# Two banks of sums, two groups in turn, keys loaded by tokens and a last group with tokens on partitions, in a fused attention and expert kernel

## The chip, the cores and the metric

One core of one Trainium2 chip. The metric is the device time of one execution in microseconds (us), lower is better. The profile's span, from the first to the last instruction, is 1.8 to 1.9 us shorter than that time.

## The reference

A polynomial-sketch attention without softmax feeds an expert layer with ELU. Sizes: 4 batches, 4 heads, 1088 tokens, head size 32, sketch size 8; 4352 tokens of 128 features into 2048 hidden units and back, all float32 (the sketches and the expert weights arrive as 64-bit floats and are rounded on the chip).

```python
def phi(x):
    a = np.einsum('rd,bhsd->bhsr', S1, x)
    b = np.einsum('rd,bhsd->bhsr', S2, x)
    return np.einsum('bhsi,bhsj->bhsij', a, b).reshape(*x.shape[:-1], r * r)
q_p, k_p = (phi(q), phi(k))
kv = np.einsum('bhsf,bhsd->bhfd', k_p, v)
z = np.sum(k_p, axis=2)
num = np.einsum('bhsf,bhfd->bhsd', q_p, kv)
den = np.einsum('bhsf,bhf->bhs', q_p, z)[..., None] + 1e-06
# ... (num / den), heads joined to 128 features = x; then
h = x @ w_in
g = np.where(h > 0.0, h, np.exp(np.minimum(h, 0.0)) - 1.0)
return (g @ w_out).astype(np.float32)
```

## The kernel before

Tokens go through in 9 groups: eight of 512 tokens and a last one of 256. For each group and each of 8 pairs of weight blocks, TensorE computes two hidden blocks (`mm1`, tile `h`), ScalarE and VectorE form ELU (`elu_a`, `elu_d`, tiles `e`, `gg`), and two steps later TensorE adds two products to the group's sum (`mm2`, tile `o`). One such pass is a step. The keys of a batch (`KF`, `KO`, `KA`), the queries of a group (`q1` to `q5`) and the rounding of the weights (`RA`, `RB`, `RC`) are hung between the steps. The kernel uses PSUM, the memory that matmuls write, in 8 banks: four for `h`, two for `aux`, one for `kv` (which also holds `wps`), one for `o`.

```python
def KF(b, gi):                       # key features of one group of tiles
    if gi < 2:
        abps[b] = psum.tile([P, 512], F32, name="abp", tag="aux")
    abp = abps[b] if gi < 2 else abps[b][:, 256:]      # the last tile shares the bank of gi == 1
    # ... matmuls into abp ...
    nc.scalar.copy(ab[...], abp[...])
# ...
def KA(b, gi):
    if gi == 0:
        kv_ps[b] = psum.tile([P, 4, 2 * D], F32, name="kv", tag="kv", bufs=1)
    # ... kv += kp.T @ v ...
def KZ2(b):
    wps = kv_ps[b][:, 2]
    nc.tensor.matmul(wps[:, :H * R], SX[:], zm[:]...)
    nc.vector.tensor_mul(SW[:, b, :, 2, :], wps[...], bmask...)
# ...
def mm2(g, cp, first, last):
    if first:
        ops[g] = psum.tile([P, 512], F32, name="o", tag="o", bufs=1)
    # ... two matmuls accumulate into ops[g] ...
def fin1(g, last):                   # partial sums of groups 0 and 1 go to SBUF and are added
    # ...
def fin2(g):                         # last group: transposes back to tokens
    # nc.tensor.transpose x2, nc.scalar.copy, two output DMAs, both from nc.sync
# ...
seg = [(g, r) for r in (range(0, 2), range(2, 4), range(4, NP)) for g in range(2)]
seg += [(g, range(NP)) for g in range(2, NQ)]
```

Of the kernel before, what the change touches and what calls it, by code (L numbers as in the profile page):

```python
# [27 lines left out]
def kernel(  # L28
# [50 lines left out]
    def load_v(eng, b):  # L79
        for u in range(2):  # L80
# [59 lines left out]

    hd["k", 0] = work.tile([P, 2, NT, D], F32, name="hd_k", tag="hd_k")
    for i, eng in enumerate((nc.sync, nc.scalar)):
        eng.dma_start(hd["k", 0][64 * i:64 * i + 64].rearrange("p c t d -> p (c t d)"),
                      k[0, 2 * i:2 * i + 2].rearrange("h (a x) d -> (h a) (x d)", a=32))
# [3 lines left out]
    load_hd(nc.sync, "q", q, 0, 0, 8)  # L148
# [37 lines left out]
    load_v(nc.sync, 0)  # L186
# [8 lines left out]
    for b in range(1, B):  # L195
        load_hd(nc.sync, "k", k, b, 0, NT)
        load_v(nc.sync, b)
        load_hd(nc.sync, "q", q, b, 0, NT)
# [16 lines left out]
    idle = psum.tile([P, 512], F32, name="idle", tag="o", bufs=1)  # L215
# [21 lines left out]
    Sab = const.tile([FD, H, 2 * R], F32, name="Sab")  # L237
    SW = const.tile([FD, B, H, 3, R], F32, name="SW")
    keep_warm(3)
    sps = psum.tile([P, 512], F32, name="sps", tag="aux")  # L240
    nc.tensor.matmul(sps[:, :2 * R], Sx[:].rearrange("p h d -> p (h d)"), ident[:2 * R, :2 * R])
    nc.vector.tensor_mul(Sab[:], _ap(sps[:, :2 * R], [[0, H], [1, 2 * R]]), _ap(bmask[:], [[1, H], [0, 2 * R]]))  # L242
    for b in range(B):
        nc.gpsimd.tensor_copy(SW[:, b, :, :2, :].rearrange("p h x r -> p h (x r)"), Sab[:])

# [7 lines left out]

    def outer(dst, ab):

        a_, b_ = ab[:, :, 1, :], ab[:, :, 0, :]
        nc.vector.tensor_mul(dst, _ap(a_, list(a_.ap[1:]) + [[0, R]]), _ap(b_, [b_.ap[1], [0, R], b_.ap[2]]))  # L257
# [3 lines left out]
    abps, kv_ps, feats, zms, kvz = {}, {}, {}, {}, {}  # L261

    def KF(b, gi):

        if gi < 2:
            abps[b] = psum.tile([P, 512], F32, name="abp", tag="aux")
        abp = abps[b] if gi < 2 else abps[b][:, 256:]
        tiles = KG[gi]
        n = len(tiles)
        rows = P if tiles[-1] + KT < NT else 64  # L270
        for j, i in enumerate(tiles):
            for u in range(rows // 64):
                nc.tensor.matmul(abp[64 * u:64 * u + 64, j * 64:j * 64 + 64], kT[b][:, u * KT + i, :],  # L273
                                 Sab[:].rearrange("p h y -> p (h y)"),
                                 skip_group_check=True, tile_position=(0, 64 * u))
        ab = work.tile([P, 4, H, 2, R], F32, name="ab", tag="ab", bufs=3)
        nc.scalar.copy(ab[:rows, :n].rearrange("p t h x r -> p (t h x r)"), abp[:rows, :n * 64])  # L277
        feats[b, gi] = ab, rows
# [9 lines left out]
    def KA(b, gi):  # L288
# [3 lines left out]
        if gi == 0:  # L292
            kv_ps[b] = psum.tile([P, 4, 2 * D], F32, name="kv", tag="kv", bufs=1)
# [12 lines left out]
    def KC(b):  # L306

        kv = kv_ps[b][:, :2, :D + 1]
# [15 lines left out]
    def KZ2(b):  # L324
        zm = zms.pop(b)
        wps = kv_ps[b][:, 2]
# [93 lines left out]
    def q5_first():  # L420
# [3 lines left out]
        RC(0)  # L424
# [13 lines left out]
        for tt in range(2):  # L438
            nc.vector.tensor_scalar(dn[:, tt], xps[tt][:, :, D], 1e-6, None, op0=ADD)
            nc.vector.reciprocal(dn[:, tt], dn[:, tt])  # L440
            nc.vector.tensor_mul(xn[:, tt], xps[tt][:, :, :D], _ap(dn[:, tt], [[1, 8], [0, D]]))
        for tt in range(2):
# [3 lines left out]
            nc.scalar.copy(xg[0][:, 256 * tt:256 * tt + 256], q[:, :256])  # L446
            if tt == 0:
                q1(1)
# [72 lines left out]
    def mm2(g, cp, first, last):  # L521
        n = qn[g] * P
        if first:
            ops[g] = psum.tile([P, 512], F32, name="o", tag="o", bufs=1)
# [5 lines left out]
    oT = {}  # L530

    def fin1(g, last):
        n = qn[g] * P
        o = ops.pop(g)[:, :n]
        if g in oT:
            nc.vector.tensor_add(oT[g][:, :n], oT[g][:, :n], o)
            o = oT[g][:, :n]
# [168 lines left out]
```

## Time and profile before

| | before |
|---|---|
| time | 299.99 us, median of 3 (299.66 to 300.33) |
| span of the profiled run | 296.4 us |
| TensorE busy; VectorE; ScalarE | 284.5 us (96%); 168.0 (57%); 188.1 (63%) |
| first `h` matmul, first `o` matmul | 19.75 us, 28.23 us |
| first `o` to the end of the last `o` | 262.98 us |
| end of the last `o` to the end of the span | 5.2 us |

The last three rows cut the span: a **head** until the first `o`, a **body**, and a **tail**. The prediction shows the slices, the chain and the head of TensorE's timeline. One view is not shown there, TensorE's waits from 26 us to the end (engine, line and tile, then who released it: total us, how often, the longest):

```profile
PE abp L273 <- ACT ab L277: 1.4, 3, 0.5
PE otp L559 <- DVE oT L543: 0.5, 1, 0.5
PE abp L273 <- DVE kT L233: 0.3, 1, 0.3
```

So in 270 us TensorE idles for four recorded holes in the body and one in the tail. Whatever the change wins in the body, it can win only from these 1.7 us.

### The profile page before, as it was taken

What the parts mean: (1) busy time and instruction counts of PE and PEld (TensorE: products, weight loads), DVE (VectorE), ACT (ScalarE), POOL (GpSimd) and SP (SyncE); (2) the same over time, 40 slices, a digit from 0 to 9 for tenths busy, and PEclk for the clock granted to TensorE, in tenths of its full rate; (3) what the DMA queues carried; (4) which work ended last, traced back from release to release, by engine and by line L of the source; (5) the groups of instructions that cost most, each with busy time, mean ns of one, the idle gap of its engine ahead of it and who ended that gap; (6) DMA issues with size and microseconds to landing.
All of it is one profiled execution on the core that took longest, in us unless ns stands there. A gap on an engine that the chain in (4) does not pass through costs nothing.

```text
span 296.4 us, 4034 instructions
## 1 busy us (share of the span) xinstructions
PE 284.5 (96%) x1448; PEld 146.0 (49%) x1448; DVE 168.0 (57%) x296; ACT 188.1 (63%) x355; POOL 19.0 (6%) x46
## 2 busy tenths in 40 slices
PE   6879989999999999999999999999999999999993
PEld 4854444544544653445544644444444444444682
DVE  4789999964657275425457274435543554355441
ACT  2249888566467467666646557766666686667681
POOL 1110034620000010000000100000000000000000
PEclk9799999999999999999999999999999999999998
DMA  6942999220110100011001100011002000110010
GB/s 157 339 157 88 198 208 217 39 75 0 18 20 9 30 0 0 3 16 19 1 2 16 21 0 0 1 18 19 0 0 31 8 0 1 17 21 0 6 30 18
DMA packets 37907, 13.37 MB, mean 45 GB/s; under 512 B 32768, under 2 KB 35968, under 8 KB 37888
## 3 DMA queue, kind: packets, MB, share of 16 engines
q1 hardware_dynamic: 37792, 12.84, 19.9%
q10 hardware_dynamic: 96, 0.28, 0.4%
q8 instruction: 11, 0.18, 0.3%
q14 instruction: 8, 0.07, 0.1%
HBM read 10.88 MB, written 2.23 MB: 44 GB/s over the span
## 4 chain that ended last, share of the span: by engine, by line
PE 86%; DVE 8%; DMA 3%; issue 1%; ACT 1%; ACTq 0%; DVEq 0%; SPq 0%
PE o L527 38%; PE h L497 35%; PE kv L300 3%; PE abp L273 2%; PE abwp L367 2%; PE xps L475 2%; PE qtp L460 2%; DMA hd_k<-in_k_dram 2%; DVE gg L514 1%; DMA raw<-in_moe_w_out_dram 1%; DVE W L114 1%; DVE kT L233 1%; DVE raw L119 1%; DVE raw L115 1%; DVE W L101 1%
## 5 line engine op out<-in xcount | busy, mean ns | idle before, releaser
L514 DVE SCALAR_TENSOR_TENSOR gg<-e,h 128x512 f32<-128x512 f32 (+1 forms) x144 | 93.0, 654 | 101.5 <-ACT e L508 101.4
L527 PE MATMUL o<-gg,W 128*128 128x512 f32 (+1 forms) x288 | 130.3, 576 | 0.0
L497 PE MATMUL h<-xg,W 128*128 128x512 f32 (+1 forms) x288 | 128.7, 569 | 0.9 <-ACT xg L446 0.5
L506 ACT ACTIVATE e<-h 128x512 f32<-128x512 f32 (+1 forms) x144 | 81.5, 566 | 23.7 <-PE h L497 23.2
L508 ACT ACTIVATE e<-e 128x512 f32<-128x512 f32 (+1 forms) x144 | 87.3, 606 | 4.5
L497 PEld LDWEIGHTS h<-xg,W 128*128 128x128 f32 x288 | 54.4, 190 | 63.6 <-issue 54.9
L527 PEld LDWEIGHTS o<-gg,W 128*128 128x128 f32 x288 | 52.5, 190 | 52.3 <-issue 48.8
L461 ACT COPY qpT<-qtp 128x512 f32<-128x512 f32 (+1 forms) x16 | 8.3, 562 | 17.1 <-PE qtp L460 17.1
L372 ACT COPY abw<-abwp 128x384 f32<-128x384 f32 (+1 forms) x8 | 3.7, 459 | 23.7 <-PE abwp L367 23.7
L257 DVE TENSOR_TENSOR kp<-ab 128x1024 f32<-128x1024 f32 (+1 forms) x12 | 11.0, 948 | 5.4 <-ACT ab L277 5.4
L277 ACT COPY ab<-abp 128x256 f32<-128x256 f32 (+1 forms) x12 | 3.8, 317 | 12.9 <-PE abp L273 12.6
L273 PE MATMUL abp<-Sab,kT 128*64 128x64 f32 x136 | 7.1, 247 | 3.4 <-DVE Sab L242 1.4
L300 PEld LDWEIGHTS kv<-v,kp 128*64 128x64 f32 (+1 forms) x288 | 9.0, 137 | 2.6 <-issue 2.3
L300 PE MATMUL kv<-v,kp 128*64 128x33 f32 (+3 forms) x288 | 9.7, 224 | 0.0
L390 DVE TENSOR_TENSOR qp<-an,abw 128x1024 f32<-128x1024 f32 (+1 forms) x9 | 9.3, 1046 | 0.3
L273 PEld LDWEIGHTS abp<-Sab,kT 128*64 128x64 f32 x136 | 5.9, 157 | 6.7 <-issue 2.6
L460 PEld LDWEIGHTS qtp<-ident,qp 128*128 128x128 f32 x60 | 7.0, 143 | 4.4 <-issue 2.8
L486 ACT COPY xg<-xps 128x256 f32<-128x256 f32 (+1 forms) x8 | 2.9, 359 | 9.5 <-PE xps L475 9.5
L460 PE MATMUL qtp<-ident,qp 128*128 128x128 f32 x60 | 8.1, 275 | 0.8 <-DVE qp L390 0.8
L320 POOL TENSOR_TENSOR zm<-kvz,zmask 128x32 f32<-128x32 f32 x4 | 1.5, 384 | 112.8 <-issue 64.5
L106 ACT ACTIVATE W<-W,ebias 128x512 uint32<-128x512 uint32 (+1 forms) x9 | 6.0, 672 | 2.7 <-DVE W L101 2.7
L124 POOL TENSOR_TENSOR raw<-raw,tiny 128x512 f32<-128x512 f32 x4 | 5.3, 1318 | 32.0 <-DVE raw L119 31.9
(82 smaller groups left out, 125.0 us busy)
## 6 DMA issues: line engine op xcount, KB each, us to landing
raw<-in_moe_w_in_dram SPq DMA_DIRECT2D x8, 256.0 KB, 6.0
raw<-in_moe_w_out_dram SPq DMA_DIRECT2D x8, 256.0 KB, 6.1
out_dram<-ob SPq DMA_DIRECT2D x104, 16.0 KB, 1.5
hd_k<-in_k_dram SPq DMA_DIRECT2D x3, 544.0 KB, 6.1
hd_q<-in_q_dram SPq DMA_DIRECT2D x3, 544.0 KB, 3.9
v<-in_v_dram SPq DMA_DIRECT2D x12, 72.0 KB, 5.6
v<-in_v_dram SPq DMA_DIRECT2D x12, 64.0 KB, 3.8
v<-in_v_dram SPq DMA_DIRECT2D x1, 288.0 KB, 5.9
```

The costliest lines, as they stand in the source:

```text
L106: nc.scalar.activation(d, d, RELU, scale=8.0, bias=ebias[:dst.shape[0]])
L257: nc.vector.tensor_mul(dst, _ap(a_, list(a_.ap[1:]) + [[0, R]]), _ap(b_, [b_.ap[1], [0, R], b_.ap[2]]))
L273: nc.tensor.matmul(abp[64 * u:64 * u + 64, j * 64:j * 64 + 64], kT[b][:, u * KT + i, :], Sab[:].rearrange("p h y -> p (h y)"), skip_group_ ...
L300: nc.tensor.matmul(kv[64 * hp:64 * hp + 64, g2, :n], kp[:rows, j, h].rearrange("p i j -> p (i j)"), _ap(vt[b][:rows, off:off + D], [[VN - ...
L390: nc.vector.tensor_mul(qp[g][:, h], _ap(a_, list(a_.ap[1:]) + [[0, R]]), _ap(b_, [b_.ap[1], [0, R], b_.ap[2]]))
L460: nc.tensor.transpose(p[:, o:o + P], qp[g][:, r:r + 2].rearrange("p t i j -> p (t i j)"), ident[:])
L461: nc.scalar.copy(qpT[g][:, 2 * hh:2 * hh + 2, :nh, :], p[:, :2 * nh * P].rearrange("p (h m s) -> p h m s", h=2, m=nh))
L497: nc.tensor.matmul(hs[g, cp][c][:, :n], W[:, cp, c * P:c * P + P], xg[g][:, :n])
L506: nc.scalar.activation(e, hs[g, cp][c][:, :n], RELU, scale=-1.0)
L508: nc.scalar.activation(e, e, EXP, scale=-1.0)
L514: nc.vector.scalar_tensor_tensor(gs[g, cp][:, c, :n], es[g, cp][:, c, :n], -1.0, hs[g, cp][c][:, :n], op0=ADD, op1=MAX)
L527: nc.tensor.matmul(ops[g][:, :n], W[:, cp, (2 + c) * P:(3 + c) * P], gg[:, c, :n], start=(first and c == 0), stop=(last and c == 1))
```

## The change

The intent: give groups 0 and 1 a bank of sums each and take each pair of weight blocks for both in turn, so that no partial sums are moved and the rounding of the weights has twice the time per pair; start the keys on half of the tokens; take the last key tile out of the shared bank's way; reorder the start (with one warming matmul less); and let the last group come out with tokens on partitions, without transposes. The second `o` bank is taken from `kv`, which moves into the `h` banks together with `wps`.

```diff
-    hd["k", 0] = work.tile(...)          # two halves by heads, both needed by the first transpose
-    ...
+    load_hd(nc.sync, "k", k, 0, 0, KT)   # two halves by tokens
+    load_hd(nc.scalar, "k", k, 0, KT, NT)
+    load_hd(nc.sync, "q", q, 0, 0, 8)
+    load_v(0, (nc.sync, nc.scalar))
 ...
-    def KF(b, gi):
+    def KF(b, part):                     # part 1: the matmuls of gi 1 and 2, then both copies
 ...
-            kv_ps[b] = psum.tile([P, 4, 2 * D], F32, name="kv", tag="kv", bufs=1)
+            kv_ps[b] = psum.tile([P, 512], F32, name="kv", tag="h", bufs=4)[:, :4 * D]...
-        wps = kv_ps[b][:, 2]
+        wps = psum.tile([P, 512], F32, name="wps", tag="h", bufs=4)
 ...
-        RC(0)                            # in q5_first
+        round_w(round_c, 0)
+        round_w(round_d, 0)              # round_e(0) and q1(1) follow before the transposes
 ...
-            ops[g] = psum.tile([P, 512], F32, name="o", tag="o", bufs=1)
+            ops[g] = psum.tile([P, 512], F32, name="o", tag="o", bufs=2)
 ...
+    def mm2_last(cp, first, last):       # gg is stationary, W moves: tokens on partitions
+        ...
+    def fin_last():                      # a copy each on ScalarE and VectorE, an output DMA each
 ...
-    seg = [(g, r) for r in (range(0, 2), range(2, 4), range(4, NP)) for g in range(2)]
+    steps = [(g, cp) for cp in range(NP) for g in range(2)] + [(g, cp) for g in range(2, NQ) for cp in range(NP)]
 ...
-        n = NP - 2 if b == 1 else NP * (b * NT // 8 - 2) + 1
-        at(n - 1, transp, kT, "k", b, 0, NT)
+        n, m = (NP - 3, 1) if b == 1 else (NP * (b * NT // 8 - 2) + 1, 0)
+        at(n - 1 - m, transp, kT, "k", b, 0, NT)
```

More of the change, by code (lines that the diff above doesn't have):

```diff
@@ L77, in load_hd, with load_v @@
                       src[b].rearrange("h (a c t) d -> (h a) c t d", a=32, c=2)[:, :, t0:t1, :])
-    def load_v(eng, b):
-        for u in range(2):
+    def load_v(b, engs=(nc.sync, nc.sync)):
+        for u, eng in enumerate(engs):
             t0, t1 = u * KT, min(NT, u * KT + KT)
@@ L139 @@
             eng.dma_start(S16[rs, :], src)
-    hd["k", 0] = work.tile([P, 2, NT, D], F32, name="hd_k", tag="hd_k")
-    for i, eng in enumerate((nc.sync, nc.scalar)):
-        eng.dma_start(hd["k", 0][64 * i:64 * i + 64].rearrange("p c t d -> p (c t d)"),
-                      k[0, 2 * i:2 * i + 2].rearrange("h (a x) d -> (h a) (x d)", a=32))
+    load_hd(nc.sync, "k", k, 0, 0, KT)
+    load_hd(nc.scalar, "k", k, 0, KT, NT)
+    load_hd(nc.sync, "q", q, 0, 0, 8)
+    load_v(0, (nc.sync, nc.scalar))
     warm = const.tile([R, 1], F32, name="warm")
@@ L147 @@
     nc.scalar.activation(warm[:], warm[:], EXP)
-    load_hd(nc.sync, "q", q, 0, 0, 8)
     W = const.tile([P, NP, 4 * P], F32, name="W")
@@ L184, in RC @@
         round_w(round_e, i, pool)
-    load_v(nc.sync, 0)
     load_w(0, 0)
@@ L196 @@
         load_hd(nc.sync, "k", k, b, 0, NT)
-        load_v(nc.sync, b)
+        load_v(b)
         load_hd(nc.sync, "q", q, b, 0, NT)
@@ L213 @@
     nc.vector.tensor_reduce(hmask[:], ident[:].rearrange("p (x j) -> p x j", x=2), axis=AX, op=ADD)
-    idle = psum.tile([P, 512], F32, name="idle", tag="o", bufs=1)
+    idle = psum.tile([P, 512], F32, name="idle", tag="o", bufs=2)
     def keep_warm(n, cols=256):
@@ L235, with make_SX @@
     transp(kT, "k", 0, 0, KT)
+    SX = const.tile([P, FD], F32, name="SX")
+    def make_SX():
+        xps = psum.tile([P, 512], F32, name="SXps", tag="aux")
+        nc.tensor.matmul(xps[:, :FD], idr[:].rearrange("p x j -> p (x j)"), Sx[:R].rearrange("p h d -> p (h d)"))
+        nc.scalar.copy(SX[:], xps[:, :FD])
     Sab = const.tile([FD, H, 2 * R], F32, name="Sab")
@@ L241 @@
     nc.tensor.matmul(sps[:, :2 * R], Sx[:].rearrange("p h d -> p (h d)"), ident[:2 * R, :2 * R])
+    make_SX()
     nc.vector.tensor_mul(Sab[:], _ap(sps[:, :2 * R], [[0, H], [1, 2 * R]]), _ap(bmask[:], [[1, H], [0, 2 * R]]))
@@ L244 @@
         nc.gpsimd.tensor_copy(SW[:, b, :, :2, :].rearrange("p h x r -> p h (x r)"), Sab[:])
-    SX = const.tile([P, FD], F32, name="SX")
-    def make_SX():
-        xps = psum.tile([P, 512], F32, name="SXps", tag="aux")
-        nc.tensor.matmul(xps[:, :FD], idr[:].rearrange("p x j -> p (x j)"), Sx[:R].rearrange("p h d -> p (h d)"))
-        nc.scalar.copy(SX[:], xps[:, :FD])
     def outer(dst, ab):
@@ L260 @@
     kvS = const.tile([P, B, H, D], F32, name="kvS")
-    abps, kv_ps, feats, zms, kvz = {}, {}, {}, {}, {}
-    def KF(b, gi):
-        if gi < 2:
-            abps[b] = psum.tile([P, 512], F32, name="abp", tag="aux")
-        abp = abps[b] if gi < 2 else abps[b][:, 256:]
-        tiles = KG[gi]
-        n = len(tiles)
-        rows = P if tiles[-1] + KT < NT else 64
-        for j, i in enumerate(tiles):
-            for u in range(rows // 64):
-                nc.tensor.matmul(abp[64 * u:64 * u + 64, j * 64:j * 64 + 64], kT[b][:, u * KT + i, :],
-                                 Sab[:].rearrange("p h y -> p (h y)"),
-                                 skip_group_check=True, tile_position=(0, 64 * u))
-        ab = work.tile([P, 4, H, 2, R], F32, name="ab", tag="ab", bufs=3)
-        nc.scalar.copy(ab[:rows, :n].rearrange("p t h x r -> p (t h x r)"), abp[:rows, :n * 64])
-        feats[b, gi] = ab, rows
+    kv_ps, feats, zms, kvz = {}, {}, {}, {}
+    def KF(b, part):
+        abp = psum.tile([P, 512], F32, name="abp", tag="aux")
+        todo = []
+        for gi, o in ((1, 0), (2, 256)) if part else ((0, 0),):
+            tiles = KG[gi]
+            rows = P if tiles[-1] + KT < NT else 64
+            for j, i in enumerate(tiles):
+                for u in range(rows // 64):
+                    nc.tensor.matmul(abp[64 * u:64 * u + 64, o + j * 64:o + j * 64 + 64], kT[b][:, u * KT + i, :],
+                                     Sab[:].rearrange("p h y -> p (h y)"),
+                                     skip_group_check=True, tile_position=(0, 64 * u))
+            todo.append((gi, o, rows, len(tiles)))
+        for gi, o, rows, n in todo:
+            ab = work.tile([P, 4, H, 2, R], F32, name="ab", tag="ab", bufs=3)
+            nc.scalar.copy(ab[:rows, :n].rearrange("p t h x r -> p (t h x r)"), abp[:rows, o:o + n * 64])
+            feats[b, gi] = ab, rows
     def KO(b, gi):
@@ L292, in KA @@
         if gi == 0:
-            kv_ps[b] = psum.tile([P, 4, 2 * D], F32, name="kv", tag="kv", bufs=1)
+            kv_ps[b] = psum.tile([P, 512], F32, name="kv", tag="h", bufs=4)[:, :4 * D].rearrange("p (g d) -> p g d", g=2)
         kv = kv_ps[b]
@@ L306, in KC @@
     def KC(b):
-        kv = kv_ps[b][:, :2, :D + 1]
+        kv = kv_ps[b][:, :, :D + 1]
         kvz[b] = work.tile([P, 2, 2, D + 1], F32, name="kvz", tag="kvz")
@@ L441, in q5_first @@
             nc.vector.tensor_mul(xn[:, tt], xps[tt][:, :, :D], _ap(dn[:, tt], [[1, 8], [0, D]]))
+        round_w(round_e, 0)
+        q1(1)
         for tt in range(2):
@@ L445, in q5_first @@
                 nc.tensor.transpose(q[:, t * P:t * P + P], xn[:, tt, 4 * t:4 * t + 4].rearrange("p m d -> p (m d)"), ident[:])
-            nc.scalar.copy(xg[0][:, 256 * tt:256 * tt + 256], q[:, :256])
-            if tt == 0:
-                q1(1)
+            (nc.scalar.copy if tt else nc.vector.tensor_copy)(xg[0][:, 256 * tt:256 * tt + 256], q[:, :256])
     def q4(g):
@@ L528, in mm2, with fin1 @@
                              start=(first and c == 0), stop=(last and c == 1))
-    oT = {}
-    def fin1(g, last):
+    def fin1(g):
         n = qn[g] * P
         o = ops.pop(g)[:, :n]
-        if g in oT:
-            nc.vector.tensor_add(oT[g][:, :n], oT[g][:, :n], o)
-            o = oT[g][:, :n]
-        elif not last:
-            oT[g] = work.tile([P, 512], F32, name="oT", tag="oT")
-            nc.scalar.copy(oT[g][:, :n], o)
-        if last and g == NQ - 1:
-            oT[g] = work.tile([P, 512], F32, name="oT", tag="oT")
-            nc.vector.tensor_copy(oT[g][:, :n], o)
-        elif last:
-            ob = work.tile([P, 4, 2, 2, D], F32, name="ob", tag="ob", bufs=2)
-            nc.vector.transpose(ob[:].rearrange("p i u w d -> p (i u w) d"), o)
-            rows = out.rearrange("(b w y t) (q d) -> b w q y t d", b=B, w=2, t=NT, q=4)
-            for u in range(2):
-                for b, t, i, m in runs(g, u, 0, qn[g]):
-                    for w in range(2):
-                        for q_ in range(4):
-                            nc.sync.dma_start(rows[b, w, q_, :, t:t + m, :], ob[32 * q_:32 * q_ + 32, i:i + m, u, w, :])
@@ L555, in fin2 @@
-    def fin2(g):
-        n = qn[g]
-        p = psum.tile([P, 512], F32, name="otp", tag="aux")
-        for i in range(n):
-            nc.tensor.transpose(p[:, i * P:i * P + P], oT[g][:, i * P:i * P + P], ident[:])
-        o = work.tile([P, 4, P], F32, name="osb", tag="osb", bufs=1)
-        nc.scalar.copy(o[:, :n].rearrange("p t f -> p (t f)"), p[:, :n * P])
-        rows = out.rearrange("(b y t) f -> b y t f", b=B, t=NT)
-        for u in range(2):
-            for b, t, i, m in runs(g, u, 0, n):
-                nc.sync.dma_start(rows[b, :, t:t + m, :], o[64 * u:64 * u + 64, i:i + m, :])
@@ L568 @@
-    keep_warm(2)
+        ob = work.tile([P, 4, 2, 2, D], F32, name="ob", tag="ob", bufs=2)
+        nc.vector.transpose(ob[:].rearrange("p i u w d -> p (i u w) d"), o)
+        rows = out.rearrange("(b w y t) (q d) -> b w q y t d", b=B, w=2, t=NT, q=4)
+        for u in range(2):
+            for b, t, i, m in runs(g, u, 0, qn[g]):
+                for w in range(2):
+                    for q_ in range(4):
+                        nc.sync.dma_start(rows[b, w, q_, :, t:t + m, :], ob[32 * q_:32 * q_ + 32, i:i + m, u, w, :])
@@ new lines, in mm2_last @@
+    def mm2_last(cp, first, last):
+        g = NQ - 1
+        if first:
+            ops[g] = [psum.tile([P, P], F32, name="ol", tag=t, bufs=k) for t, k in (("o", 2), ("o", 2))]
+        gg = gs.pop((g, cp))
+        for a in range(4):
+            c, i = (a % 2, a // 2) if last else divmod(a, 2)
+            nc.tensor.matmul(ops[g][i][:], gg[:, c, i * P:i * P + P], W[:, cp, (2 + c) * P:(3 + c) * P],
+                             start=(first and c == 0), stop=(last and c == 1))
+    def fin_last():
+        g, n = NQ - 1, qn[NQ - 1]
+        o = work.tile([P, 2, P], F32, name="ol", tag="ol", bufs=1)
+        rows = out.rearrange("(b y t) f -> b y t f", b=B, t=NT)
+        for i, copy in enumerate((nc.scalar.copy, nc.vector.tensor_copy)):
+            copy(o[:, i, :], ops[g][i][:])
+        for u, eng in enumerate((nc.sync, nc.scalar)):
+            b, t = half_tile(g, 0, u)
+            eng.dma_start(rows[b, :, t:t + n, :], o[64 * u:64 * u + 64])
@@ L569 @@
+    keep_warm(1)
     transp(kT, "k", 0, KT, NT)
@@ L574 @@
     q1_first()
-    KF(0, 2)
-    make_SX()
     KO(0, 1)
@@ L585 @@
     q5_first()
-    mm1(0, 0, (0,))
+    mm1(0, 0)
     RA(1)
     RB(1)
-    elu_a(0, 0, 0, (0,))
+    elu_a(0, 0, 0)
     q2(1, 2)
     q4(1)
-    mm1(0, 0, (1,))
-    elu_a(0, 0, 0, (1,))
-    RC(1)
+    round_w(round_c, 1)
+    round_w(round_d, 1)
     x1 = q5(1, True)
@@ L598 @@
     elu_a(0, 0, 1, (1,))
-    mm1(0, 1)
+    round_w(round_e, 1)
+    mm1(1, 0)
     RA(2)
@@ L603 @@
         elu_d(0, 0, c)
-    for c in range(2):
-        elu_a(0, 1, c)
-    RC(2)
-    RA(3)
-    for c in range(2):
-        elu_d(0, 1, c)
-    RB(3)
-    seg = [(g, r) for r in (range(0, 2), range(2, 4), range(4, NP)) for g in range(2)]
-    seg += [(g, range(NP)) for g in range(2, NQ)]
-    steps = [(g, cp, cp == r[0], cp == r[-1]) for g, r in seg for cp in r]
+    elu_a(1, 0, 0)
+    RA(3)
+    RB(3)
+    elu_a(1, 0, 1)
+    RC(2)
+    for c in range(2):
+        elu_d(1, 0, c)
+    steps = [(g, cp) for cp in range(NP) for g in range(2)] + [(g, cp) for g in range(2, NQ) for cp in range(NP)]
     extra = {}
@@ L625, in late @@
         extra.setdefault((n, 1), []).append((f, *a))
-    for n, i in ((2, 3), (3, 4), (5, 5), (6, 6), (8, 7), (9, 8)):
+    for i in range(3, NP + 1):
+        n = 2 * i - 4
         if i > 3:
@@ L632 @@
     for b in range(1, B):
-        n = NP - 2 if b == 1 else NP * (b * NT // 8 - 2) + 1
-        at(n - 1, transp, kT, "k", b, 0, NT)
+        n, m = (NP - 3, 1) if b == 1 else (NP * (b * NT // 8 - 2) + 1, 0)
+        at(n - 1 - m, transp, kT, "k", b, 0, NT)
         for i in range(3):
-            at(n, KF, b, i)
-            at(n + (i > 0), KO, b, i)
-            at(n + 2, KA, b, i)
-        late(n + 2, KC, b)
-        late(n + 2, KZ1, b)
-        late(n + 2, KS, b)
-        at(n + 4, KZ2, b)
-        at(n + 3, transp, qT, "q", b, 0, NT)
+            if i < 2:
+                at(n, KF, b, i)
+            at(n + (1 + m) * (i > 0), KO, b, i)
+            at(n + 2 + m, KA, b, i)
+        late(n + 2 + m, KC, b)
+        late(n + 2 + m, KZ1, b)
+        late(n + 2 + m, KS, b)
+        at(n + 4 + m, KZ2, b)
+        at(n + 3 + m, transp, qT, "q", b, 0, NT)
     for g in range(2, NQ):
@@ L650 @@
         at(n + 6, q5, g)
-    done = {}
     N = len(steps)
-    for n in range(N + 4):
-        if 2 <= n < N:
-            g, cp, first, last = steps[n]
+    for n in range(2, N + 2):
+        if n < N:
+            g, cp = steps[n]
             mm1(g, cp)
@@ L659 @@
             f(*a)
-        if 2 <= n < N:
+        if n < N:
             elu(g, cp, 0)
-        if 2 <= n < N + 2:
-            g2, cp2, first, last = steps[n - 2]
-            if last:
-                mm2(g2, cp2, first, last)
-                fin1(g2, cp2 == NP - 1)
-                if cp2 == NP - 1 and g2 == NQ - 1:
-                    done[n + 2] = g2
-        if 2 <= n < N:
             elu(g, cp, 1)
@@ L672 @@
             f(*a)
-        if 2 <= n < N + 2 and not last:
-            mm2(g2, cp2, first, last)
-        if n in done:
-            fin2(done[n])
+        g, cp = steps[n - 2]
+        if g == NQ - 1:
+            mm2_last(cp, cp == 0, cp == NP - 1)
+        else:
+            mm2(g, cp, cp == 0, cp == NP - 1)
+            if cp == NP - 1:
+                fin1(g)
+    fin_last()
 _INS = ['q', 'k', 'v', 'S1', 'S2', 'moe_w_in', 'moe_w_out']
```

## The prediction

> **What bounds the kernel now.** I first read the page's slices, in tenths busy:
>
> ```profile
> PE   6879989999999999999999999999999999999993
> DVE  4789999964657275425457274435543554355441
> PEclk9799999999999999999999999999999999999998
> ```
>
> TensorE is full from the fourth slice to the last but one (one slice is 296.4 / 40 = 7.4 us). VectorE is full only in slices 4 to 8, where the expert weights are rounded. A busy row does not prove that TensorE sets the time, so I read the chain of work that ended last:
>
> ```profile
> 93.86 1.72 PE o L527 x4
> 95.58 1.72 PE h L497 x4
> 97.29 2.34 PE kv L300 x72
> ...
> 288.61 2.60 PE o L527 x12
> 291.21 0.02 issue
> 291.24 0.44 DVE oT L543
> 291.67 0.04 issue
> 291.72 0.45 PE otp L559 x2
> 292.17 0.02 issue
> 292.19 0.37 ACT osb L561
> ```
>
> From 44.4 to 291.2 us every piece of the chain is TensorE's. Its unit is 4 records in 1.72 us (two 512-column matmuls of two records each): 1.72 + 1.72 = 3.44 us for one pair of one full group. 8 groups x 8 pairs x 3.44 + 8 pairs x 1.72 for the half group = 234 us, plus keys, queries and transposes. The change removes none of these. What can move is therefore (a) when TensorE becomes continuous, (b) holes in it afterwards, (c) the 5.2 us after the last `o`. TensorE's own timeline of the head shows (a):
>
> ```profile
> 19.75 1.12 PE L497 MATMUL h<-xg,W 128*128 128x512 f32 x2 [0.48 <-ACT xg L446]
> 21.64 1.23 PE L460 MATMUL qtp<-ident,qp 128*128 128x128 f32 x8 [0.76 <-DVE qp L390]
> ...
> 24.70 3.70 PE L497 MATMUL h<-xg,W 128*128 128x512 f32 x8 [0.37 <-DVE W L127]
> 28.23 1.88 PE L527 MATMUL o<-gg,W 128*128 128x512 f32 x4
> ...
> 42.44 1.15 PE L273 MATMUL abp<-Sab,kT 128*64 128x64 f32 x32 [0.29 <-DVE kT L233]
> 44.05 0.33 PE L273 MATMUL abp<-Sab,kT 128*64 128x64 f32 x2 [0.46 <-ACT ab L277]
> ```
>
> From 24.7 us TensorE has two holes, 0.29 and 0.46 us, so the partial sums and the rounding of pairs 2 to 7 cost TensorE almost nothing already. The waits of TensorE from 44 to 291 us have one line, `PE abp L273 <- ACT ab L277`, 0.47 us at 89.9 and at 155.7.
>
> **What the Trainium skill says.** "Perfetto Trace Analysis", Identifying the Most-Contended Engine, calls matmul busy share a poor measure of the distance to roofline; I use cadence and holes instead, and the even 1.72 us supports that. "TensorE: Matmul & The Clock Gate", Architectural detail, says that VectorE and ScalarE are strict FIFO and that TensorE may pull only weight loads ahead; the trace agrees (at 95 to 100 us ScalarE idles 5.05 us behind a copy while newer `h` tiles lie ready). The same page, What's actually happening, says that an idle array falls to half clock: here the granted clock is 0.50 from 8 to 10 us, after TensorE idled 5.74 to 7.19. "DMA: Bandwidth & Descriptors", Issuing engines are not separate DMA queues, says that a second issuing engine saves only issue time; the two output issues at the end take 1.20 us on one queue.
>
> **Part 1, keys by tokens, head reordered.** The first key transpose now starts on half the tokens of all heads while the second half is still landing. Now: last half lands 6.2, two transposes, first dense key matmul 7.81. After: I take 6.0 for the second half, its transpose ends 6.7, key matmuls from 6.8 at the same half clock (16 records x 0.063 = 1.0), copy, first `kp` at 9.5 instead of 10.5. VectorE then runs `kp` (2.69 for three), RA(0) and `qp` (1.2) to 12.4 instead of 13.4. The key sums overlap that and end about 12.4 instead of 14.1, since the last key tile and SX no longer stand behind the queries. Then, on VectorE: kvz 12.7, round_c and round_d of W0 (0.45+0.33+0.47) 13.95, SW 14.05, qT 14.75; `x0ps` ends 15.7 (2.0 us from 13.7); two dn/xn groups to 16.55; round_e 16.95; xg copies 17.4 and 17.7. **First `h` at about 17.75 instead of 19.75.**
>
> From there: q2(1) on VectorE 17.7 to 20.3 (it took 2.63), round_c and round_d of W1 to 22.15 (0.72+0.47+0.75), xg(1) 22.5, round_e 23.15, RA(2) 23.35, two elu_d 24.55 (0.6 each), RA(3) 24.9, RC(2) (1.6) 26.5. mm2(0,0) needs RC(2): it starts at **26.5 instead of 28.23**. By then the same three pairs of `h` are done in both kernels (17.75 to 19.5, 22.55 to 24.3, 24.3 to 26.0). So of the 2.0 us, 0.3 is lost again to rounding: **-1.7 us**.
>
> **Part 2, key matmuls before both copies.** The wait of 0.46 to 0.47 us is the last two `abp` records asking for a bank that ScalarE is still reading. Issued ahead of both copies they don't wait: 3 x about 0.5 with refill = **-1.5**. The 0.29 us wait for kT goes as its transpose moves earlier: **-0.3**.
>
> **Part 3, two `o` banks, groups in turn.** This removes two copies on ScalarE (1.2 us) and four adds on VectorE (4 x 0.68 = 2.7), and asks for one rounded pair every two steps (6.88 us) where a pair costs VectorE 2.24 to 2.93 and its two steps' elu_d 2.5. It gives slack to VectorE, but TensorE had no hole there: **0**, beyond holding the earlier start.
>
> **Part 4, the bank that pays for it.** `kv` and `wps` now take slots of `h`. For batches 2 and 3 the slot of `wps` is the one read last by elu_d of the step before. On the timelines of before, from 104 to 111 us:
>
> ```profile
> 106.33 1.31 DVE L233 STREAM_TRANSPOSE qT<-hd_q 128x1088 f32<-128x1088 f32 x1
> 107.35 0.30 PE L327 MATMUL kv<-zm,SX 128*128 128x32 f32 x2
> 107.56 1.25 DVE L514 SCALAR_TENSOR_TENSOR gg<-e,h 128x512 f32<-128x512 f32 x2
> ```
>
> TensorE comes to `wps` at 107.35, but VectorE, held by q2 and the qT transpose, finishes the first of those two elu_d only at 108.2: a new hole of 0.85 us, and the same at 173.2: **+1.7**. For `kv` itself the needed elu_d ends 1.0 us before (96.25 against 97.22), and for batch 1 no q2 stands there: 0.
>
> **Part 5, last group.** Its mm2 becomes 4 x 128 columns for 2 x 256. Transposes of 128 columns run 8 records in 0.87 us, about the 0.86 of now; I add **+0.3** over 8 steps for weight loads. After the last matmul, copy + transpose + copy (0.44+0.45+0.37, and 0.08 of issue) become one 128-column copy on each of two engines (about 0.3), and the two issues go in parallel (-0.6, an estimate from 1.20 for two): **-1.6**.
>
> **Part 6, keys of batch 1.** Their transpose moves to step 3, so VectorE asks at about 31.9. The load goes out after W1's and W0's raw buffers are free: 28.87 now, about 27.4 then, and lands 5.1 to 6.8 us later, so 32.5 to 34.2. VectorE waits 0.7 to 2.3 us, and the elu_d behind it is needed by TensorE at 35.1: **+0.5** of a range 0 to 1.1.
>
> Sum: -1.7 - 1.5 - 0.3 + 1.7 + 0.3 - 1.6 + 0.5 = **-2.6 us**. As the head could also escape the half clock, I take -3.0: 299.99 - 3.0 = **297.0 us**, 1.0% faster.
>
> **Rivals.** *The head pays more.* If the key matmuls run at full clock and all VectorE links shrink, up to another 1.5 us go, and without the `wps` holes 1.7 more: about 293.8. For it: the chain to 28 us is nearly all VectorE and key loading. Against: VectorE's list before mm2(0,0) is as long as before, only reordered. *The banks become the bound.* With three `h` slots around each `kv`, every step there could hole, 3 batches x 1 to 2 us: 299 to 300. For it: `h` is double buffered exactly and VectorE runs a step late. Against: outside q2 and transposes elu_d ends at least 0.2 us ahead. *Loads decide.* The second half of v joins the keys on the other queue while the 16 engines are full (share 1.01 from 4 to 6 us); if keys land 1 us later, the start gains 0.7 instead of 1.7: 298.
>
> **Range and chances.** The head may be off by 1.2 either way, `wps` by 0.9, batch 1's keys by 0.6, the rest by 0.7: together about 1.8, so 297.0 with 294.4 to 299.2 for 8 in 10. Faster by over 2% means below 294.0: it needs all gains and no new hole, 0.10. Slower by over 2% needs 6 us of new holes: 0.02. Within 2%: 0.88.
>
> **What would show it.** First `h` near 17.8 and first `o` near 26.5 us. No wait of `abp` on the ab copies. Two holes of some 0.85 us ahead of `wps` with elu_d as releaser; if they are missing, slots are handed out otherwise than I think. A wait of VectorE for hd_k near 32 us. From last `o` to the end 3.6 us instead of 5.2. The prediction fails if the new `h` slots stall TensorE elsewhere, or if the last group's 128-column matmuls run slower than 0.11 us each.

## The result, and the profile after

The changed kernel took **296.49 us** (median of 4 runs, 296.19 to 298.13) against 299.86 us of the kernel before (the three runs above and a fourth). The ratio is 0.9897, with a 95% interval of 0.9858 to 0.9935. Ratios here are the mean time of one kernel's fast runs over that of the other's of the same rounds, so not quite the ratio of the medians. All outputs were correct, in this and every run below.

| | before | after | predicted |
|---|---|---|---|
| first `h` | 19.75 | 17.93 | 17.75 |
| first `o` | 28.23 | 26.84 | 26.5 |
| first `o` to the end of the last | 262.98 | 263.58 | 263.7 (sum of its terms) |
| tail | 5.2 | 3.9 | 3.6 |
| span | 296.4 | 294.4 | 293.8 (296.4 less the 2.6) |

The body became **longer**: taken together, the change won nothing between the first and the last `o`. TensorE's waits from 26 us to the end, in the changed kernel, beside the list of before:

```profile
PE wps L326 <- DVE gg L514: 1.7, 2, 0.8
PE h L497 <- DVE gg L514: 0.4, 1, 0.4
PE o L527 <- DVE W L127: 0.2, 1, 0.2
```

All the old holes are gone, and new ones of nearly the same sum stand there. The chain of waits shows one of the two `wps` holes (start, us, what; pieces follow one another):

```profile
104.04 1.31 DVE qT L230
105.35 0.58 DVE gg L514
105.93 0.14 issue
106.06 0.38 PE wps L326 x2
106.44 0.91 PE qtp L460 x8
```

VectorE transposes queries, then finishes an ELU, and only then is the bank free that `wps` takes. In the kernel before, `wps` stood in the bank of `kv` and followed `h` at once. By cadence, counted from start to start, the hole is 1.0 us: the `h` before it starts at 103.33, its four records take 1.72, and `wps` starts at 106.06.

The head, from TensorE's timeline (start, busy us, engine, line, operation, tiles, records, and in brackets the idle time before and its releaser):

```profile
6.32 1.15 PE L270 MATMUL abp<-Sab,kT 128*64 128x64 f32 x32 [0.28 <-DVE kT L230]
8.43 0.69 PE L399 MATMUL abqp<-Sab,qT 128*64 128x64 f32 x16 [0.95 <-DVE qT L230]
9.79 2.46 PE L299 MATMUL kv<-v,kp 128*64 128x64 f32 x72 [0.67 <-DMA v<-in_v_dram]
...
17.93 1.98 PE L497 MATMUL h<-xg,W 128*128 128x512 f32 x4 [0.46 <-ACT xg L448]
...
26.84 1.98 PE L527 MATMUL o<-gg,W 128*128 128x512 f32 x4 [0.19 <-DVE W L127]
```

The keys start 1.5 us earlier (6.32 for 7.81) and at full rate (32 records in 1.15 us; before, 29 in 1.83). Then the first queries (0.95) and `v` (0.67) are waited for, and part of the lead is lost to them. The tail, from the chain of waits:

```profile
287.73 2.69 PE ol L551 x24
290.45 0.29 DVE ol L559
```

One copy of 0.29 us stands where a copy, a transpose and a copy stood.

### The profile page after: what moved, and what is told of

The parts are those of the page before. It is cut to its first block, busy times and chain, and to the rows that moved or that the text cites. A ratio compares the mean times of both kernels' runs of the same rounds, so it can differ in the third digit from the quotient of the medians.

```text
span 294.4 us, 4086 instructions
## 1 busy us (share of the span) xinstructions
PE 283.2 (96%) x1476; PEld 145.4 (49%) x1476; DVE 166.4 (57%) x293; ACT 186.6 (63%) x352; POOL 16.8 (6%) x46
## 4 chain that ended last, share of the span: by engine, by line
PE 84%; DMA 5%; DVE 4%; ACT 3%; issue 2%; SPq 1%
PE h L497 35%; PE o L527 34%; PE kv L299 3%; PE xps L475 2%; PE ol L551 2%; DMA v<-in_v_dram 2%; DMA hd_k<-in_k_dram 2%; PE abwp L366 2%; PE qtp L460 2%; DVE gg L514 2%; PE abp L270 1%; DVE qT L230 1%; ACT e L508 1%; ACT e L506 1%; PE x0ps L432 1%
## 5 line engine op out<-in xcount | busy, mean ns | idle before, releaser
L527 PE MATMUL o<-gg,W 128*128 128x512 f32 x256 | 122.4, 600 | 0.2 <-DVE W L127 0.2
L527 PEld LDWEIGHTS o<-gg,W 128*128 128x128 f32 x256 | 46.4, 190 | 51.7 <-issue 49.5
L255 DVE TENSOR_TENSOR kp<-ab 128x1024 f32<-128x1024 f32 (+1 forms) x12 | 12.0, 1033 | 3.8 <-ACT ab L276 3.8
L551 PEld LDWEIGHTS ol<-W,gg 128*128 128x128 f32 x64 | 8.1, 192 | 0.3
L551 PE MATMUL ol<-W,gg 128*128 128x128 f32 x64 | 8.1, 275 | 0.0
L475 PE MATMUL xps<-qpT,kvS 64*32 64x128 f32 (+2 forms) x200 | 7.6, 298 | 0.2 <-ACT qpT L461 0.2
L475 PEld LDWEIGHTS xps<-qpT,kvS 64*32 64x32 f32 x200 | 4.1, 105 | 6.1 <-ACT e L508 5.3
```

The lines of the kernel that those rows point to most:

```text
L255: nc.vector.tensor_mul(dst, _ap(a_, list(a_.ap[1:]) + [[0, R]]), _ap(b_, [b_.ap[1], [0, R], b_.ap[2]]))
L475: nc.tensor.matmul(xp[w][D * h:D * h + D, :nh * P].rearrange("p (m s) -> p m s", s=P)[:, m0:m0 + m, s], kvS[64 * w:64 * w + 64, b, h, :], ...
L527: nc.tensor.matmul(ops[g][:, :n], W[:, cp, (2 + c) * P:(3 + c) * P], gg[:, c, :n], start=(first and c == 0), stop=(last and c == 1))
L551: nc.tensor.matmul(ops[g][i][:], gg[:, c, i * P:i * P + P], W[:, cp, (2 + c) * P:(3 + c) * P], start=(first and c == 0), stop=(last and c ...
```

## The experiments

Twelve experiments ran, in three calls on three chips, 5 rounds each. The first letter says what was edited: `a` the changed kernel, `b` the kernel before with one part of the change alone.

| kernel | time, us (runs) | before, same call | ratio | first `o` | body | tail |
|---|---|---|---|---|---|---|
| a_wps | 294.29 (293.7 to 295.4) | 297.98 | 0.9877 | 26.75 | 261.24 | 3.9 |
| a_k1 | 295.18 (295.1 to 295.4) | 297.98 | 0.9902 | 26.70 | 262.80 | 3.9 |
| a_both | 293.22 (292.9 to 293.7) | 297.98 | 0.9833 | 27.16 | 260.73 | 3.9 |
| a_kheads | 297.72 (296.3 to 298.4) | 297.98 | 0.9984 | 27.90 | 263.88 | 3.9 |
| b_kf | 296.45 (295.6 to 297.5) | 300.03 | 0.9908 | 28.75 | 261.62 | 5.2 |
| b_tail | 299.10 (296.6 to 299.3) | 300.03 | 0.9973 | 30.22 | 263.21 | 3.8 |
| b_head | 296.35 (296.1 to 296.6) | 300.03 | 0.9904 | 26.43 | 262.97 | 5.2 |
| b_banks | 300.73 (300.2 to 303.4) | 300.03 | 1.0077 | 28.38 | 265.40 | 5.2 |
| a_same | 296.42 (295.8 to 297.2) | 298.29 | 0.9925 | 26.76 | 263.90 | 3.9 |
| b_nobanks | 293.71 (293.6 to 294.4) | 298.29 | 0.9835 | 26.83 | 261.82 | 3.9 |
| a_both2 | 293.21 (292.8 to 293.5) | 298.29 | 0.9814 | 26.62 | 260.74 | 3.9 |
| b_warm | 297.94 (fast runs 297.0 to 298.3) | 298.29 | 0.9964 | - | - | - |

The last three columns come from each kernel's one profiled run; body and tail are the parts defined above. The kernel before does not repeat well: of its 37 timed runs over the four calls 21 lie from 297.0 to 298.4 us and 16 from 299.7 to 300.6, and how many of each differs by call (4 of 4 high in the first, then 1, 7 and 4 of 11); the reason seems to lie in the head (see b_warm). So medians against it scatter by over 2 us between calls, and **the body is the sharper measure of a part**. It comes from one profile each: the changed kernel's own body was 263.58 and 263.90 in two profiles, so differences under 0.3 us say little.

### a_wps: the wps matmul two steps later

```diff
-        at(n + 4 + m, KZ2, b)
+        at(n + (4 + m if b == 1 else 6), KZ2, b)
```

> The changed kernel with one edit: the small matmul wps of batches 2 and 3 is issued two steps later (step n+6 in place of n+4), when the h slot that it takes has long been read; nothing is added or removed. Bank theory (the kv and wps tiles in the h banks cost the change two holes of 0.85 us ahead of wps): both holes go, no wait of wps on gg is left, and the time falls by 1.7 us against the changed kernel, to about 294.8 (ratio to before near 0.983). Rival (the two holes are filled by something else, since VectorE is late anyway and the next h would wait instead): the wait moves to an h or qtp matmul and the time falls by under 0.5 us.

The body fell by 2.34 us (263.58 to 261.24), the time to 294.29. Both `wps` waits are gone from the list of waits and no new one took their place. The rival falls. The hole is TensorE waiting for a PSUM bank that VectorE reads late, and 2.0 of the 2.34 us is what the two holes measure by cadence; most of the rest is the hole behind the keys of batch 1 (see a_k1), 0.32 us in this run for 0.57. a_both, which differs from a_k1 by this edit alone, is 1.96 us below it (293.22 for 295.18).

### a_k1: keys of batch 1 ahead of the last two weight pairs

```diff
     for cp in range(2, NP):
+        if cp == NP - 2:
+            load_hd(nc.sync, "k", k, 1, 0, NT)
         load_w(cp, 0)
         load_w(cp, 1)
 ...                                     # and the later loop skips the keys of batch 1
```

> The changed kernel with one edit: the keys of batch 1 are loaded ahead of the last two pairs of expert weights, whose raw buffers come free late, so the load goes out near 13 us and not at 27.7. Load theory: VectorE's wait of 2.08 us for hd_k at 32 to 34 us goes, and with it the hole of 0.41 us ahead of h at 36.1; the time falls by 0.3 to 0.6 us. Rival (VectorE's wait hides more: all of its 2.08 us comes back since rounding is the limit until 50 us): the time falls by over 1.2 us. A second rival: the last two weight pairs now arrive too late and the time rises.

In the changed kernel the wait stood on VectorE's timeline, and behind it on TensorE's:

```profile
34.12 1.36 DVE L230 STREAM_TRANSPOSE kT<-hd_k 128x1088 f32<-128x1088 f32 x1 [2.08 <-DMA hd_k<-in_k_dram]
```

```profile
36.10 1.98 PE L497 MATMUL h<-xg,W 128*128 128x512 f32 x4 [0.41 <-DVE gg L514]
```

Loaded early, both go. The body fell by 0.78 us, where 0.3 to 0.6 was expected; the hole is 0.57 us by cadence (the `o` before starts at 33.81 and takes 1.72). VectorE's 2.08 us did not come back as a whole: it had slack, TensorE's hole is what counts. The second rival, late weights, falls too: no new wait on them appeared. By time the edit gave more: a_both is 1.07 us below a_wps, which lacks this edit alone, where their bodies differ by 0.5. That is under the 1.2 us of the first rival, but the other half is not explained.

### a_both and a_both2: both edits

> Both edits of the two kernels before it. If both are true holes of TensorE and independent, the gains add: 1.7 + 0.4 = 2.1 us below the changed kernel, about 294.4 us, ratio to before near 0.982. If TensorE is refilled elsewhere, less than 1 us in all.

The body is 260.73, 2.85 below the changed kernel, near the sum of the two (2.34 + 0.78). TensorE's waits from 26 us to the end are then a single line, 0.2 us at the first `o` itself:

```profile
PE o L530 <- DVE W L127: 0.2, 1, 0.2
```

> The changed kernel with wps two steps later and the keys of batch 1 loaded early, a second time, now in one call with the unedited changed kernel and with the kernel without the banks. Theory: 2.1 us or a little more below the changed kernel, so 293.0 to 294.4; and against the kernel without the banks it shows what the banks are worth once their two costs are paid back: 0 by the prediction (equal within 0.5 us), or the gain of the banks if it is faster.

In one call with the unedited changed kernel, 293.21 against 296.42 us: 3.2 us less, more than the 2.1 expected.

### a_same: the changed kernel again

> The changed kernel, unedited, as the control on the chip of this call (the calls before ran on two chips, and the kernel before runs in two or three clusters, 297.2, 298.1 and 300.1 us). Expected 296.2 to 296.7 us in most runs; against the clustered kernel before the ratio comes out between 0.987 (before near 300) and 0.995 (before near 297.5).

296.42 us in the median, as expected, though only 2 of its 6 runs lie between 296.2 and 296.7. Its body is 0.3 us longer than in the first profile, because the hole behind the keys of batch 1 was 0.90 us by cadence for 0.57. Its gain over the kernel before is 1.9 us here and was 3.4 in the first call. The changed kernel stayed; the kernel before moved, from near 300 to 298.29 in the median.

### a_kheads: the changed kernel with the old loading of the first keys

```diff
-    load_hd(nc.sync, "k", k, 0, 0, KT)
-    load_hd(nc.scalar, "k", k, 0, KT, NT)
+    hd["k", 0] = work.tile([P, 2, NT, D], F32, name="hd_k", tag="hd_k")
+    # two contiguous halves by heads, as in the kernel before
```

> The changed kernel, but the keys of batch 0 are loaded again as in the kernel before, as two contiguous halves by heads, both of which the first transpose needs. Theory of the prediction (keys by tokens start the chain about 0.8 us earlier): first dense key matmul about 1 us later, near 7.3, and the time rises by 0.6 to 1.0 us. Rival, from the trace after (VectorE then waits 1.3 us for the first queries until 7.57, and TensorE 0.67 us for v until 9.79, so these loads hide the keys): the keys land later but the first h matmul stays within 0.2 us of 17.93 and the time does not move by more than 0.3 us.

TensorE's head in this kernel:

```profile
7.72 1.93 PE L272 MATMUL abp<-Sab,kT 128*64 128x64 f32 x32 [0.29 <-DVE kT L232]
9.44 1.07 PE L401 MATMUL abqp<-Sab,qT 128*64 128x64 f32 x16
10.51 2.77 PE L301 MATMUL kv<-v,kp 128*64 128x64 f32 x72
```

The first `h` comes at 19.00 in place of 17.93, the first `o` at 27.90 in place of 26.84, and the time, 297.72, is 1.3 above a_same (another chip, so that difference is rough). The rival, that the waits for queries and `v` hide the keys, falls: in these profiles loading by tokens is worth about 1.1 us of the head, most of what the head wins (1.39). The keys also ran at half rate here (32 records in 1.93 us, granted clock 0.50 from 7.81 to 11.22 us), so the 1.1 us holds the later start and the slower clock together.

### b_kf: key matmuls ahead of both copies, alone

The edit is the changed kernel's `KF` and its two calls, put into the kernel before.

> The kernel before with one part of the change: the matmuls of the last key tile are issued ahead of both copies out of that bank. Theory: the three waits of abp on the ab copies (0.46, 0.47, 0.47 us) go and the time falls by 1.4 to 1.6 us, to about 298.3, plus up to 0.3 in the head where the queries' matmuls no longer stand ahead of the last key tile. Rival: TensorE then meets the copies one instruction later (o or h waits) and under 0.5 us is won.

The body fell by 1.36 us, about as expected. But one wait is new, at 61.4 us:

```profile
61.38 1.12 PE L528 MATMUL o<-gg,W 128*128 128x512 f32 x2 [0.55 <-DVE oT L537]
```

TensorE, now earlier after its first `o`, meets the single `o` bank while VectorE still adds a partial sum. By cadence each of the three holes was 0.69 us (from the first `abp` record to the next `o` 1.87 to 1.88 us before, 1.16 to 1.19 now), 2.1 us in all, and the new hole took 0.72 of it back (from `wps` to `o` 0.86 us for 0.14): the rival was right in part. In the kernel before, that add ended at 60.77 us and the `o` came at 60.83, so the hole was 0.06 us away, and its profile showed it. This also shows what the second `o` bank is good for. The median (296.45) exaggerates, as the kernel before was in its upper cluster for most of this call.

### b_tail: the last group with tokens on partitions, alone

The edit is `mm2_last` and `fin_last`, the second accumulator in an `aux` bank.

> The kernel before with one part of the change: the last group's second matmul with tokens on partitions (its second accumulator takes an aux bank), no transposes at the end, the two output issues on two queues. Theory: 8 steps cost 0.03 us more each (+0.25), and from the last o to the end 3.95 us in place of 5.2 (-1.25): the time falls by 1.0 us, to about 298.9. Rival: the end is set by the landing of the last transfer, not by copies and issues, and the time falls by under 0.4.

The body grew by 0.23 us, the tail shrank from 5.2 to 3.8: 1.2 less in all. The runs lie in two clusters, two at 296.6 and 297.2 and four at 299.1 to 299.3; the upper one is about 1.0 below the upper cluster of the kernel before in this call (300.0 to 300.6), and two runs are too few to place the lower. As expected; the rival, that the last transfer alone sets the end, falls.

### b_head: loads and start, alone

> The kernel before with one part of the change: the loads of the first keys and v over two queues, SX early, the reordered start of the first two groups (round_e late, queries of group 1 before the transposes), one warming matmul less; the order of groups, the banks, the key matmuls of later batches and the end stay. Theory: first h near 18.3 in place of 19.75 (the last key tile still stands behind the queries), first o about 1.2 us earlier, the time falls by 1.0 to 1.5 us. Rival (VectorE's rounding sets the first o whatever comes before): first h is earlier but the first o and the time move by less than 0.5 us.

The first `h` came at 18.07 and the first `o` at 26.43, 1.8 us earlier, a little more than expected; the body is untouched (262.97 for 262.98). The time fell by 3.7 us in the median, because the kernel before was mostly in its upper cluster, while all 6 runs here lie within 0.4 us at 296.1 to 296.6: no upper cluster showed. Which of this part's edits does that was not separated.

### b_banks: two banks and the turn-taking, alone

The edits are the two `o` banks, `kv` and `wps` in `h`, the order of steps, the rounding's places and the start from the first `h` on.

> The kernel before with one part of the change: two banks of sums, groups 0 and 1 in turn, no partial sums, rounding spread over all 16 steps, and therefore kv and wps in h banks; loads, key matmuls, head up to the first h, and the end stay. Theory of the prediction: spreading the rounding is worth 0 to TensorE, the two wps holes cost 1.7 us and the early keys of batch 1 about 0.4, so the time RISES by 1.5 to 2.2 us, to about 301.7. Rival (this is the part that makes the change pay): the time falls by 0.5 us or more.

TensorE's waits from 26 us to the end:

```profile
PE wps L327 <- DVE gg L514: 1.7, 2, 0.8
PE abp L273 <- ACT ab L277: 1.4, 3, 0.5
PE otp L552 <- DVE oT L537: 0.5, 1, 0.5
PE h L497 <- DVE gg L514: 0.5, 1, 0.5
PE o L527 <- DVE W L127: 0.2, 1, 0.2
```

The body grew by 2.42 us: by cadence the two `wps` holes (2.0) and the one behind the early keys (0.65), less the wait for kT (0.36), which is gone. The time is 300.73, 0.8% above the kernel before (interval 0.2 to 1.3%); that is 0.7 us in the medians, less than the predicted 1.5 to 2.2, as the kernel before was mostly in its upper cluster and 4 of the 6 runs here were not in theirs. The two profiled runs, both with the key sums at full rate, are 2.55 us apart (300.85 and 298.30, in different calls). The part that gives the change its name **costs** time where it stands alone, as predicted.

### b_nobanks: everything but the banks

> The kernel before with three parts of the change at once (head and loads, key matmuls ahead of both copies, last group with tokens on partitions) but not the fourth: one bank of sums with partial sums, groups 0 and 1 in the order of before, kv and wps in their own bank. Theory (the two banks are worth nothing to TensorE and cost 1.7 us ahead of wps and 0.4 us at the early keys): from the first o to the end of the last o 261.9 us in place of 263.6, first o near 26.4, and the time is 1.5 to 2.3 us below the changed kernel of the same call, about 294.5. Rival (the banks and the turn-taking earn something that only shows once the head is short, as rounding then presses): new waits of o or h on W or gg between 26 and 50 us, and the time is equal to the changed kernel's or above.

293.71 us, 2.7 below a_same, a little more than the expected 2.3; the body is 261.82, the expected 261.9, though the first `o` came at 26.83 and not near 26.4 (the profiled run, 294.39, is the slowest of the six). So the changed kernel would have been faster without its main part. The rival does not appear: no wait on weights after 26 us. The one wait that stays in its body besides the keys' is again `o` on the partial sums (0.6 us). Against it, a_both2 tells what the banks are worth once their two debts are paid: 293.21 for 293.71, **0.5 us**, and a body 1.1 us shorter. The prediction's 0 was too low by that much. By cadence the 1.1 us is the `o` hole (0.72) and the wait for kT (0.36, gone because the keys of batch 1 are transposed earlier). About half of it is lost again at the start: from the first `h` to the first `o` every fast profile with the turn-taking takes 8.9 to 9.1 us, every one without 8.35 to 8.49. a_both2 is the fastest kernel, 1.9% below the kernel before.

### b_warm: more warming matmuls in the kernel before

```diff
-    keep_warm(2)
+    keep_warm(4)
```

> The kernel before with two more warming matmuls ahead of the second key transpose, so that TensorE is not idle from 5.7 to 7.2 us. Clock theory (that idle stretch is what puts the key matmuls or the key sums at half rate, 2.46 us against 4.30 for the 72 records of kv, and so makes the clusters of 297.2, 298.1 and 300.1 us): the slow cluster vanishes and the runs lie at 297 to 298. Rival (the half rate comes from a window that runs freely and was decided before, as one trace with half rate from 4.7 us on suggests): the clusters stay, and the time is not below 297; where the warming itself runs at half rate it ends near 8 us and delays the keys by some 0.3 us.

What makes the clusters can be read from the 72 records of the key sums. Kernel before, profiled run of 298.3 us:

```profile
11.60 2.46 PE L300 MATMUL kv<-v,kp 128*64 128x64 f32 x72
```

b_kf, profiled run of 297.45 us:

```profile
11.16 3.42 PE L301 MATMUL kv<-v,kp 128*64 128x64 f32 x72
```

b_tail, profiled run of 299.08 us:

```profile
11.73 4.30 PE L300 MATMUL kv<-v,kp 128*64 128x64 f32 x72
```

The same work runs at full rate, at half rate for a part, or nearly all at half rate, and the first `o` follows (28.23, 28.75, 30.22). That stretch of slow matmuls accounts for the upper cluster of b_tail; that it is also the cause in the runs of the kernel before at 300 us, of which no profile exists, is inferred.

Where the slow stretch comes from is another question, and the traces speak against the theory as it was put. The warming matmuls of the same start, first in the kernel before, then in b_tail:

```profile
4.61 1.13 PE L219 MATMUL idle<-some 128*128 128x256 f32 x4
4.63 2.08 PE L219 MATMUL idle<-some 128*128 128x256 f32 x4
```

In b_tail, and likewise in b_kf, TensorE ran at half rate before the idle stretch that the theory blames. The first clock event of the packed trace, a grant of full speed, comes at 16.47 us in b_tail, at 13.30 in b_kf and at 4.46 in the kernel before (there with half speed again from 7.87 to 11.28), and the spacing of the matmuls changes at these times. Nor is such a stretch enough: b_nobanks idles 1.53 us until 8.98 and stays at full rate.

With two more warming matmuls the five fast runs lie at 297.0 to 298.3, without one near 300, where the kernel before in the same call had 4 of 11. Were nothing changed, five such runs in a row would still have a chance of (7/11)^5, 10%. So it is supported that a slow stretch makes the upper cluster; what decides when full speed is first granted is **not settled**, and the rival is not refuted. The profiled run of b_warm (337.4 us, granted clock 0.852) is not used.

In the changed kernel the slow stretch does little harm where it was seen: in a_same, 33 key records took 2.08 us, half rate, and in the first profile 32 took 1.15, yet the first `h` came at 17.85 and 17.93. There the loads of queries and `v` set the pace at that point.

## Why the prediction was right

It said 297.0 us (294.4 to 299.2), 1.0% faster; it was 296.49, 1.0% faster by the ratio. By its steps:

- **The body is bound by TensorE, only holes count.** Right: every edit moved the body by the holes that it made or removed, to within the 0.3 us by which a body repeats, and VectorE's 2.08 us wait for keys counted only 0.57.
- **Head, -1.7.** It was -1.39. Here two errors cancelled. The keys landed earlier than the assumed 6.0 us and ran at full rate, and the lead was then lost to waits for the first queries and `v`, which the prediction had only as a rival ("Loads decide"). The head alone (b_head) is worth 1.8. The turn-taking takes the difference back between the first `h` and the first `o`, where the prediction reckoned 0.3 us for rounding and 0.4 to 0.6 was lost. One sum on the way is off by 0.09 us (20.3 + 0.72 + 0.47 + 0.75 is 22.24, not 22.15), which changes nothing.
- **Key matmuls, -1.5, and the wait for kT, -0.3.** The mechanism is shown by b_kf, the sizes were too small: by cadence three holes of 0.69 and one of 0.36 went, -2.4 together. With +2.0 for `wps`, +0.57 for the keys of batch 1 and +0.23 for the last group this gives +0.4 for the body, where +0.60 was measured. Alone, the first gives only 1.36, since the single `o` bank takes 0.72 back.
- **Two banks, 0.** Too low: 0.5 us of time once the bank debts are paid. "TensorE had no hole there" was read from the profile of before, where the holes at the keys had delayed TensorE enough to hide the one at `o`, by 0.06 us.
- **wps, +1.7.** The holes, their number, their places and their releaser came as said, 0.85 us each in the list. By cadence they cost 1.0 each, as the idle time of the list starts only at a matmul's modelled end. The same error made the gain at the keys too small, so that the body as a whole came out right (263.7 for 263.58) by luck.
- **Keys of batch 1, +0.5.** Right: VectorE waited 2.08 us (0.7 to 2.3 was said), TensorE 0.57 by cadence.
- **Last group, +0.3 and -1.6.** +0.23 and -1.3. The copies shrank by 1.0 us, and the two issues did go in parallel (0.56 and 0.57 us for 1.20); but the rest of the tail, the landing and the end, grew from 2.6 to 3.0 us, which the prediction had as unchanged.

The terms of the change as measured give -1.39 + 0.60 - 1.3 = -2.1 us, which is the difference of the two profiled runs (298.30 and 296.19). The median of the first call shows 3.4, since all runs of the kernel before there but the profiled one lay in its upper cluster. So the closeness of 297.0 to 296.49 is partly luck: the fair size of the change against the kernel before is between 1.9 us (last call) and 3.4, depending on how many of its runs fall in that cluster. The allowance of 0.4 us for an escape from the half clock named the right thing, if the upper cluster is the slow clock as b_warm makes likely, and was small for it.

## What to carry to other kernels

Where one engine is full, list its holes before a change and ask of every buffer that moves who reads its new slot last, and when: here one engine's strict order put a 1.3 us transpose ahead of the read that freed a bank. A hole can hide behind an earlier one, so a buffer that looks idle can gain value once other holes are closed. Measure parts by a stretch that the scatter of the start doesn't touch.

## What the Trainium skill lacked or had wrong

- "TensorE: Matmul & The Clock Gate", What's actually happening, gives a return to full rate after one busy window of some 3.4 us. In b_tail full speed was first granted at 16.47 us, though in the 11.8 us before it, from the warming matmuls at 4.63 us on, the profile has TensorE idle for only 0.95 us; the key sums in between took 4.30 us for 2.46.
- The same page, Seeing it yourself, warns that clock events in traces can be unreliable. Here no event was found wrong, but a stretch without events misleads: the trace of b_tail has none before 16.47 us, and the profile's view fills that stretch with a granted clock of 1.00 while the key sums take 1.75 times as long. Until the first event the cadence of a known matmul is the better reading.
- The same page, Back-to-back issue gap, has figures per matmul without float32 (another page counts the passes of a float32 matmul, none times one): here 4 records of 512 columns take 1.72 us, and 8 of 128 columns 0.89 us in the last group.
- "Perfetto Trace Analysis", Optimization Strategy, says that consistent bubbles can mean too few buffers. The `wps` holes agree (0.85 us at both batches), but the remedy was none more: two steps' delay of one matmul closed them. The section does not say that such a bubble can belong to one tile alone, whose slot another engine reads late.
- "DMA: Bandwidth & Descriptors", Issuing engines are not separate DMA queues, calls the saved issue time small. At the tail it was 0.6 us, beside 1.3 us by which the whole tail shrank (two issues in 1.20 us on one queue, 0.56 and 0.57 side by side on two).
